# One ring of weight tiles for the whole second MLP, another order of operations inside a step, and last stores from two queues

## The chip, the cores and the metric

The kernel runs on one core of a Trainium2 chip. The metric is the device time of one execution in microseconds; the time given for a kernel is the median of its runs. Everything is computed in 32-bit floats. The engines are named as the profile names them: PE is TensorE, which multiplies matrices, PEld its weight loads; DVE is VectorE, ACT is ScalarE, POOL is GpSimd; SP is SyncE, whose queue (SPq) issues the DMAs.

## What is computed

An attention over memory slots, then two MLPs one behind the other. Cut to what matters:

```python
# q, k, v: 8 batches x 8 heads x 576 x 64; phi: 8 x 8 x 576 x 32
a = softmax(phi, axis=2)
k_m, v_m = einsum('bhsm,bhsd->bhmd', a, k), einsum('bhsm,bhsd->bhmd', a, v)
x = softmax(q @ k_m.T / 8) @ v_m            # brought to 4608 tokens x 512
h = x @ w_in                                # 512 x 2048
x = maximum(0.01 * h, h) @ w_out            # 2048 x 512
gate = sigmoid(x @ w_gate)                  # 512 x 1536
out = (gate * (x @ w_val)) @ w2_out         # 1536 x 512, result 4608 x 512
```

## The kernel before, in words

Every factor of a product is split into a high and a low part of TensorE's 32-bit format, and a product is the sum of three matmuls: high by high, low by high, high by low. The subtraction that gives the low part runs on VectorE or GpSimd, the copy that gives the high part on ScalarE.

The work has two stages. In the first, 256 steps go over 8 batches, 2 halves of 288 tokens and 16 blocks of 128 columns of the first MLP. One step of the loop over `steps` (L1354) holds, in this order: the split of an earlier block's activation (`fin`, L188 and L189), the first product of the block two steps ahead (`m1_in`, L836, and its activation L840), the operations of the attention units that are due (`unit_parts`), one tick of preparation, the units' work on TensorE (`ts_`), the weights of a later batch (`vw_pair`, L806), the second product (`m1_out`, L857), and the units' loads (`ls`). A unit is half of the heads of one batch; a table (`SCHED["chain"]` and its like) says in which step, counted from the unit's first, each of its parts is due. Among the parts: `v1` and `v2` take a maximum (L502, L515, L518); `v4` sums the exponentials in two operations on VectorE (L553, L555) and `t4` uses the sum on TensorE (L564, L573); `v5x` copies the result off with ScalarE (L603); `v10m` scales on GpSimd (L738), with its factor from the reciprocal L731.

The preparation is, in the first 30 steps, a tick that rewrites the first MLP's weights. From step 30 on it is the stash: the second MLP's weights are loaded, brought to a rounded form (L218, L222, L228 on ScalarE, L232 and L242 on VectorE, L250 on GpSimd), combined into seven blocks as Strassen's scheme wants them (L324 to L331), split (L337, L343), and stored to two DRAM tensors: `gvs` for `w_gate` and `w_val`, `w2s` for `w2_out`. The helper `run` takes a list of generators and goes around: one operation of the first, one of the second, and so on, until all are empty. Since engines work in the order in which operations are issued, this order is the order on each engine. The stash is the last generator of the list.

In the second stage the tokens are done in five pairs of blocks (480, 480, 448, 448 and 448 tokens wide). For a pair, three rounds (`th`) have each two column blocks (`j`), and for each of these one group of seven products for the gate and one for the value (`m2_group`, L1006, six matmuls a product). Between the rounds stands `m2_out` (L1142): 14 sums of products, (k, e) with k from 0 to 6 and e 0 or 1, each of six matmuls too. In what follows an operation is one such set of six matmuls with its tile of weights. A round's `m2_out` is issued behind the first group of the next round, the last round's behind its own four groups. Loads of the next pair's x (`x_load`, L907) are issued behind the first round's groups.

Weights come from DRAM through SP's queue. There are two sets of tiles. Five `wt` tiles of 512 KB hold two operations' weights each for `m2_group` and are refilled after the second one (`w_load`, L940). Four `ring` tiles of 256 KB serve `m2_out` and are refilled after each operation (`w2_load`, L952). Both wait for the matmuls that read the old content.

Each result of an `m2_out` operation is added to its sum on VectorE (L1152), or copied by ScalarE the first time (L1150); four PSUM banks take turns. In the plain order `OUT_SEQ` a bank comes again after four operations. The very last `m2_out` has an order of its own, `OUT_END`. After the last round the sums are transposed on VectorE (L1125) in chunks of 256 and 192 tokens and stored (`store`, L1182), four DMAs to a chunk and half; these operations wait in a list, `lazy`, from which a few are taken per `m2_out` operation: two in the last `m2_out`, one or two elsewhere. In the last `m2_out` two chunks of one half are stored once (4, 1) is done, the others after (6, 1), which is its last operation.

Of the kernel before, what the change touches and what calls it, by code (L numbers as in the profile page):

```python
# [119 lines left out]
def tile_kernel(  # L120
# [13 lines left out]
    nc = tc.nc  # L134
# [21 lines left out]
    NOP = 7  # L156
    IN_AT = IN_SEQ = (0, 2, 1, 3, 4, 5, 6)
    OUT_SEQ = [(k, e) for k in (0, 2, 1, 5, 4, 3, 6) for e in range(2)]
    OUT_END = [
        (0, 0), (2, 0), (1, 0), (0, 1), (5, 0), (2, 1), (4, 0), (1, 1), (3, 0), (5, 1), (6, 0), (4, 1), (3, 1), (6, 1),  # L160
    ]
    NOPS = NF2 * NOP
    SCALE = 1.0 / float(D) ** 0.5

# [16 lines left out]
    def f32(ap):  # L181
        return ap.bitcast(F32)
# [691 lines left out]
    xr = []  # L874
    xt = []
    xo = {}
    w_free = []
    w_at = {}
    w_next = [0]
    ops = []  # L880
    ring = []
    r_at = []
    sums = []
    banks = []
    stage2 = []
# [47 lines left out]
        t, h = xo[k, a], PAIRS[n][1]  # L933
        eng.tensor_sub(t[:, 1, :h], x_operand(n, k, a), f32(t[:, 0, :h]))  # L934

    def w_load():
        while w_free and w_next[0] < len(PAIRS) * NOPS // 2:
            m = w_next[0] % (NOPS // 2)
            t = w_at[w_next[0]] = w_free.pop(0)
            nc.sync.dma_start(out=f32(t), in_=gvs[:, 2 * m:2 * m + 2].rearrange("p o l a f -> p (o l a f)"))  # L940
            w_next[0] += 1

    def out_seq(n, th):
        return OUT_END if (n, th) == (len(PAIRS) - 1, NTH - 1) else OUT_SEQ

    r_next = iter([(th, e, k) for n in range(len(PAIRS)) for th in range(NTH) for k, e in out_seq(n, th)])

    def w2_load(t):
        x = next(r_next, None)
        if x:  # L950
            th, e, k = x
            nc.sync.dma_start(out=f32(t), in_=w2s[:, th, e, k])  # L952
            r_at.append(t)

    def out_open():
        for _ in range(TH // 2):
            ops.append([wtile("wo", [P, 2, 512], F32R, "op") for _ in range(NOP)])
        for _ in range(2):
            t = wtile("wo", [P, 2, TH // 2, 2, P], F32R, "ring")
            ring.extend(t[:, i] for i in range(2))  # L960
        for t in ring:
            w2_load(t)
        sums.extend(wtile("vw", [P, 2, 512], F32, "sum") for _ in range(4))
        banks.extend(ps_acc.tile([P, 512], F32, tag="acc", name="oacc") for _ in range(4))
        t = gp.tile([P, 2, 1024], F32, tag="ghl", name="turned", bufs=1)
        ts_ = [t[:, 0], t[:, 1], gp.tile([P, 1024], F32, tag="obuf", name="turned", bufs=1)]
        stage2.extend(t.rearrange("p (b q r) -> p b q r", q=4, r=32) for t in ts_)
# [24 lines left out]

    def m2_group(n, th, j, val):
        h = PAIRS[n][1]
        o0 = n * NOPS + NOP * (TH * th + 2 * j + val)
        direct = th == NTH - 1 and j == TH // 2 - 1

        def prod(k, bank, start):
            m, e = divmod(o0 + IN_AT[k], 2)
            w = w_at[m].rearrange("p (o l a f) -> p o l a f", o=2, l=2, a=2)[:, e]  # L1000
            i = 0
            for a in range(2):
                x = xo[k, a]
                for l, r in ((0, 0), (1, 0), (0, 1)):

                    nc.tensor.matmul(  # L1006
                        bank, w[:, l, a, :], x[:, r, :h], start=(start and i == 0), stop=(i == 5),
                        skip_group_check=not start,
                    )
                    i += 1  # L1010
            if e == 1:
                w_free.append(w_at.pop(m))
                w_load()

        def sg_tile():
            n_tmp[1] += 1
            return sgt[n_tmp[1] % len(sgt)][:, :h]

        def op_hi(k, x):
            return lambda: nc.scalar.copy(ops[j][k][:, 0, :h], x)  # L1020

        def op_lo(k, x):
            t = ops[j][k]
            return lambda: nc.vector.tensor_sub(t[:, 1, :h], x, f32(t[:, 0, :h]))  # L1024

        def sub(d, x, y):
            return lambda: nc.vector.tensor_sub(d, x, y)  # L1027

        def gate(s, c):
            return lambda: nc.scalar.activation(s, c, AF.Sigmoid)  # L1030

        def gated(s, c):
            return lambda: dve.tensor_mul(s, s, c)  # L1033

        def add(d, x, y):
            return lambda: dve.tensor_add(d, x, y)  # L1036

        def copy(d, x):
            return lambda: nc.scalar.copy(d, x)  # L1039

        dve = nc.vector
        turns = 0 if val else 2
        if val:
            b11, b12, b21, b22 = (sgs.pop(x) for x in range(4))
        else:
            s11, s12, s21, s22 = (sgs.setdefault(x, sg_tile()) for x in range(4))
        c11, c22, c12, r = (tmp(h) for _ in range(4))
        if val:
            t1, t2, t3, t4 = b11, tmp(h), b12, b21
        y = ps_a.tile([P, 512], F32, tag="a", name="ps_y")[:, :h]  # L1050
        prod(0, y, True)
        read(copy(c11, y), turns=turns)
        yield
        z = ps_h.tile([P, 512], F32, tag="h", name="ps_z")[:, :h]
        prod(2, z, True)
        read(copy(c22, z), turns=turns)
        yield
        prod(1, y, False)
        read(copy(c12, y), turns=turns)
        yield  # L1060
        x = ps_h.tile([P, 512], F32, tag="h", name="ps_x")[:, :h]
        prod(3, x, True)
        read(add(c11, x, c11), turns=turns)
        if val:
            gated(b11, c11)()
            after(1, op_hi(0, b11), op_lo(0, b11))
        else:
            after(1, gate(s11, c11))
        yield
        prod(4, y, False)  # L1070
        if val:
            read(copy(r, y), add(c22, r, c22), gated(b22, c22), turns=turns)
            if direct:
                op_hi(5, b22)()
            else:
                after(1, op_hi(5, b22))
        else:
            read(copy(r, y), add(c22, r, c22), turns=turns)
            after(1, gate(s22, c22))
        yield  # L1080
        prod(5, z, False)
        read(add(c12, z, c12), turns=turns)
        if val:
            gated(b12, c12)()
            sub(t1, b12, b11)()
            if direct:
                op_hi(2, t1)()
        else:
            after(1, gate(s12, c12))
        yield  # L1090
        prod(6, y, False)
        if not val:
            read(turns=turns)
            after(1, gate(s21, y))
        elif direct:
            read(gated(b21, y), turns=turns)
            op_lo(2, t1)()
            sub(t2, b22, t1)()
            op_hi(1, t2)()
            op_hi(3, b21)()  # L1100
            after(1, op_lo(1, t2), op_lo(5, b22))
            after(2, sub(t3, b22, b12), op_hi(4, t3))
            after(3, op_lo(3, b21), sub(t4, b21, t2), op_hi(6, t4))
            after(4, op_lo(4, t3))
            after(5, op_lo(6, t4))
        else:
            read(gated(b21, y), turns=turns)
            sub(t2, b22, t1)()
            after(1, op_hi(2, t1), op_hi(3, b21), op_lo(2, t1), op_lo(3, b21), op_lo(5, b22))
            after(2, op_hi(1, t2), sub(t3, b22, b12), op_lo(1, t2))  # L1110
            after(3, op_hi(4, t3), sub(t4, b21, t2))
            after(4, op_lo(4, t3))
            after(5, op_hi(6, t4))
            after(6, op_lo(6, t4))
        yield
# [3 lines left out]
    def m2_out(n, th, between):  # L1119
# [8 lines left out]

        def stored(t, x, m, st):
            f = lazy.pop()  # L1130
            lazy.append(lambda: (f(), store(t0 + t * h + x, m, st)))

        chunks = [(0, 256), (256, h - 256)]
        st = {}
        for k, e in out_seq(n, th):
            start = k in (0, 2, 3)
            b = banks[e if k in (0, 1, 4, 6) else 2 + e][:, :h]
            w = r_at.pop(0)
            i = 0
            for j in range(TH // 2):  # L1140
                for l, r in ((0, 0), (0, 1), (1, 0)):
# [2 lines left out]
                        skip_group_check=not start,  # L1144
                    )
                    i += 1
            w2_load(w)
            o = sums[SUM_OF[k]][:, e, :h]
            if th == 0 and k in (0, 2, 1, 6):
                read(lambda: nc.scalar.copy(o, b), turns=1)  # L1150
# [26 lines left out]
        n_st[0] += 1  # L1177
        return stage2[n_st[0] % len(stage2)]

    def store(n0, m, o):  # L1180
        for g in range(4):
            nc.sync.dma_start(  # L1182
                out=out[n0:n0 + m, P * g:P * g + P].rearrange("(b p) d -> p b d", p=32),
                in_=o[32 * g:32 * g + 32, 0:m // 32].rearrange("p b q r -> p b (q r)"),
            )


    with tc.manual_schedule():
# [154 lines left out]
            early.setdefault(6 + n, []).append((x_hi, (0, IN_SEQ[n // 2], n % 2)))  # L1343
            early.setdefault(7 + n, []).append((x_lo, (0, IN_SEQ[n // 2], n % 2, nc.vector)))

        def w_open():
            w_free.append(wtile("vw", [P, 2 * PC], F32R, "wt"))
            w_load()

        for n in range(5):  # L1350
            early.setdefault(4 if n == 0 else 16 + 2 * n, []).append((w_open, ()))
        first = m2_group(0, 0, 0, 0)
        held = None
        for i, (b, hf, fc) in enumerate(steps):  # L1354
# [19 lines left out]
                    convs[0].load()  # L1374
                    convs[1].load()
            else:
                vs.append(stash(i - i0 - 1))
            run(vs)
            for f, u in ts_:
                f(u)  # L1380
# [79 lines left out]
```

## Time and profile before

| | us |
|---|---|
| median of 3 runs | 1603.97 |
| lowest and highest | 1602.0, 1604.19 |
| the profiled execution | 1595.83 |
| its span, first to last instruction | 1594.1 |
| PE busy in it | 1530.8 (96%) |
| PEld busy in it | 1380.9 (87%) |
| DVE, ACT, POOL busy | 954.5, 820.8, 450.6 |

The profile is that of one execution. Busy time is the time in which an engine had an instruction running; matmuls overlap one another, so a busy PE isn't PE at its peak. "Idle before" an instruction is the time its engine did nothing ahead of it, and the releaser behind the arrow is what ended that. The first stage ends at about 784 us, the second with the last matmul near 1584 us.

### The profile page before, as it was taken

How to read it: one execution, taken by the hardware profiler on the slowest of the kernel's cores; microseconds unless marked ns; L12 is line 12 of the kernel's file. 1: busy time of each engine (PE TensorE's matmuls, PEld its weight loads, DVE VectorE, ACT ScalarE, POOL GpSimd, SP SyncE). 2: the span in 40 equal slices, each digit the busy share in tenths (PEclk: the TensorE clock that was granted, in tenths of full speed). 3: DMA queues.
4: the chain of work that ended last, by engine and by line, in shares of the span. 5: the costliest groups of instructions: out<-in, count | busy, mean ns of one | idle time of the engine just before them, and what ended most of it. 6: DMA issues, size and time to landing. Idle time of an engine off the chain costs nothing.

```text
span 1594.1 us, 28286 instructions
## 1 busy us (share of the span) xinstructions
PE 1530.8 (96%) x10508; PEld 1380.9 (87%) x10508; DVE 954.5 (60%) x1732; ACT 820.8 (51%) x1846; POOL 450.6 (28%) x445
## 2 busy tenths in 40 slices
PE   5789999999999999999999999999999999999997
PEld 2677888989999998999988888888999898989996
DVE  6886555556555556513065677558755875686466
ACT  5885555656566565645453355425543554255432
POOL 2986354444545444433200030002100200030000
PEclk8899999999999999999999999999999999999999
DMA  9823555544656565312276668666877687768774
GB/s 307 279 53 87 145 163 160 162 135 148 175 161 192 147 180 160 107 49 81 90 267 201 205 202 276 215 205 203 272 245 214 210 279 234 215 212 262 217 215 122
DMA packets 247529, 297.04 MB, mean 186 GB/s; under 512 B 98400, under 2 KB 172640, under 8 KB 247392
## 3 DMA queue, kind: packets, MB, share of 16 engines
q1 hardware_dynamic: 247392, 295.24, 60.4%
q8 instruction: 83, 1.36, 0.3%
q14 instruction: 54, 0.44, 0.1%
HBM read 243.27 MB, written 51.90 MB: 185 GB/s over the span
## 4 chain that ended last, share of the span: by engine, by line
PE 73%; DVE 5%; ACT 3%; DMA 2%; issue 1%; SPq 0%; DVEq 0%; ACTq 0%
PE ps_y L1006 18%; PE acc L857 17%; PE oacc L1142 13%; PE ps_z L1006 9%; PE ps_h L836 8%; PE ps_x L1006 5%; PE ps_vw L806 1%; DMA ring<-w2s 1%; DVE op L1024 1%; DVE sum L1152 1%; PE ps_kv L573 1%; DMA gvs<-hl 1%; DVE sg L1027 1%; DMA w2s<-hl 0%; DVE sg L1033 0%
## 5 line engine op out<-in xcount | busy, mean ns | idle before, releaser
L857 PE MATMUL acc<-ghl,wo 128*128 128x288 f32 x3072 | 463.9, 300 | 6.3 <-ACT obuf L866 2.2
L857 PEld LDWEIGHTS acc<-ghl,wo 128*128 128x128 f32 x3072 | 421.9, 189 | 32.9 <-issue 13.4
L1006 PE MATMUL ps_y<-xo,wt 128*128 128x448 f32 (+1 forms) x1440 | 332.3, 371 | 0.0
L189 POOL TENSOR_TENSOR ghl<-grs,ghl 128x288 fp32r<-128x288 f32 x250 | 217.7, 872 | 338.1 <-ACT ghl L188 244.9
L1006 PEld LDWEIGHTS ps_y<-xo,wt 128*128 128x128 f32 x1440 | 270.1, 188 | 30.3
L1142 PE MATMUL oacc<-op,ring 128*128 128x448 f32 (+1 forms) x1260 | 270.2, 372 | 4.1 <-DMA ring<-w2s 2.4
L1142 PEld LDWEIGHTS oacc<-op,ring 128*128 128x128 f32 x1260 | 234.6, 188 | 37.2 <-DVE sum L1152 3.8
L1039 ACT COPY tmp<-ps_y 128x448 f32<-128x448 f32 (+1 forms) x180 | 98.1, 545 | 267.1 <-PE ps_y L1006 267.1
L840 ACT ACTIVATE grs<-ps_h 128x288 f32<-128x288 f32 x256 | 105.7, 413 | 250.0 <-PE ps_h L836 228.7
L836 PE MATMUL ps_h<-at_hi,vw 128*128 128x288 f32 x1024 | 214.0, 297 | 3.6 <-ACT vw L188 2.8
L934 POOL TENSOR_TENSOR xo<-xr,xo 128x448 fp32r<-128x448 f32 (+1 forms) x28 | 38.4, 1404 | 594.4 <-DMA ring<-w2s 285.1
L836 PEld LDWEIGHTS ps_h<-at_hi,vw 128*128 128x128 f32 x1024 | 166.2, 190 | 5.0 <-ACT vw L188 3.6
L1006 PE MATMUL ps_z<-xo,wt 128*128 128x448 f32 (+1 forms) x720 | 169.8, 371 | 0.0
L1152 DVE TENSOR_TENSOR sum<-oacc,sum 128x448 f32<-128x448 f32 (+1 forms) x170 | 106.7, 634 | 97.5 <-PE oacc L1142 96.2
L836 PE MATMUL ps_h<-at_lo,vw 128*128 128x288 f32 x512 | 151.5, 296 | 0.0
L1006 PEld LDWEIGHTS ps_z<-xo,wt 128*128 128x128 f32 x720 | 135.1, 188 | 15.2
L1036 DVE TENSOR_TENSOR tmp<-ps_x,tmp 128x448 f32<-128x448 f32 (+1 forms) x60 | 38.1, 635 | 183.3 <-PE ps_x L1006 183.3
L1020 ACT CAST op<-sg 128x448 fp32r<-128x448 f32 (+1 forms) x180 | 103.4, 579 | 74.6 <-DVE sg L1027 44.7
L188 ACT CAST ghl<-grs 128x288 fp32r<-128x288 f32 x256 | 111.6, 436 | 2.0
L1024 DVE TENSOR_TENSOR op<-sg,op 128x448 fp32r<-128x448 f32 (+1 forms) x180 | 111.9, 645 | 0.5
L818 DVE TENSOR_TENSOR vw<-ps_vw,vw 128x256 fp32r<-128x256 f32 x112 | 39.7, 418 | 106.5 <-ACT vw L816 106.5
L836 PEld LDWEIGHTS ps_h<-at_lo,vw 128*128 128x128 f32 x512 | 96.9, 189 | 0.0
(173 smaller groups left out, 1755.6 us busy)
## 6 DMA issues: line engine op xcount, KB each, us to landing
wt<-gvs SPq DMA_DIRECT2D x210, 512.0 KB, 4.3
ring<-w2s SPq DMA_DIRECT2D x210, 256.0 KB, 2.9
gvs<-hl SPq DMA_DIRECT2D x84, 256.0 KB, 2.3
w2s<-hl SPq DMA_DIRECT2D x42, 256.0 KB, 2.4
x2s<-obuf SPq DMA_DIRECT2D x15, 576.0 KB, 3.6
win<-in_moe_w_in_dram SPq DMA_DIRECT2D x16, 512.0 KB, 10.0
wo_bits<-in_moe_w_out_dram SPq DMA_DIRECT2D x16, 512.0 KB, 10.4
q<-in_q_dram SPq DMA_DIRECT2D x224, 36.0 KB, 2.9
```

What stands on the lines that cost most here:

```text
L188: nc.scalar.copy(hi, raw)
L189: eng.tensor_sub(lo, raw, f32(hi))
L818: nc.vector.tensor_sub(w[:, 1, g], x, f32(w[:, 0, g]))
L836: nc.tensor.matmul(p[:, :HALF], w, x, start=(n == 0), stop=(n == 3 * NG - 1))
L840: nc.scalar.activation(gr, p[:, :HALF], AF.Prelu, alpha=0.01)
L857: nc.tensor.matmul(a[d][:, :HALF], w[:, ds_], x, start=(open_ and n == 0), stop=(close and n == 2),)
L1006: nc.tensor.matmul(bank, w[:, l, a, :], x[:, r, :h], start=(start and i == 0), stop=(i == 5), skip_group_check=not start,)
L1020: return lambda: nc.scalar.copy(ops[j][k][:, 0, :h], x)
L1024: return lambda: nc.vector.tensor_sub(t[:, 1, :h], x, f32(t[:, 0, :h]))
L1039: return lambda: nc.scalar.copy(d, x)
L1142: nc.tensor.matmul(b, w[:, j, l, :], ops[j][k][:, r, :h], start=(start and i == 0), stop=(i == 5), skip_group_check=not start,)
L1152: read(lambda: nc.vector.tensor_add(o, b, o), turns=2 if end and last else 1)
```

## The change

Three things are changed.

- The second MLP's weights all go through one ring. Where five tiles of 512 KB and four of 256 KB stood, there are 14 tiles of 256 KB in the same memory (ten from the five places tagged `vw`, four from the two tagged `wo`). One stream lists all operations in the order in which they are issued, products and sums of products mixed; each operation takes the oldest tile, and behind its matmuls that tile is loaded with the next content of the stream.
- In a step of the first stage with a stash, `run` first issues all operations of the units, and then the stash's by itself.
- `OUT_END` is dropped: the very last `m2_out` goes in the plain order. Its stores are issued in turn from SP and ScalarE, two DMAs of each chunk on either.

```diff
-    OUT_END = [
-        (0, 0), (2, 0), (1, 0), (0, 1), (5, 0), (2, 1), (4, 0), (1, 1), (3, 0), (5, 1), (6, 0), (4, 1), (3, 1), (6, 1),
-    ]
...
-    def w_load():
-        while w_free and w_next[0] < len(PAIRS) * NOPS // 2:
-            m = w_next[0] % (NOPS // 2)
-            t = w_at[w_next[0]] = w_free.pop(0)
-            nc.sync.dma_start(out=f32(t), in_=gvs[:, 2 * m:2 * m + 2].rearrange("p o l a f -> p (o l a f)"))
-            w_next[0] += 1
...
-    def w2_load(t):
-        x = next(r_next, None)
-        if x:
-            th, e, k = x
-            nc.sync.dma_start(out=f32(t), in_=w2s[:, th, e, k])
-            r_at.append(t)
+    def stream(n):
+        for th in range(NTH):
+            for j in range(TH // 2):
+                for val in range(2):
+                    o = NOP * (TH * th + 2 * j + val)
+                    for x in range(NOP):
+                        yield gvs[:, o + x].rearrange("p l a f -> p (l a f)")
+                    if th > 0 and (j, val) == (0, 0):
+                        yield from stream_out(th - 1)
+        yield from stream_out(NTH - 1)
+
+    def stream_out(th):
+        for k, e in OUT_SEQ:
+            yield w2s[:, th, e, k].rearrange("p j l f -> p (j l f)")
+
+    w_next = iter([x for n in range(len(PAIRS)) for x in stream(n)])
+
+    def w_load(t):
+        x = next(w_next, None)
+        if x is not None:
+            nc.sync.dma_start(out=f32(t), in_=x)
+            w_at.append(t)
+
+    def w_open(tag):
+        t = wtile(tag, [P, 2, 512], F32R, "wt")
+        for i in range(2):
+            w_load(t[:, i])
...
         for _ in range(2):
-            t = wtile("wo", [P, 2, TH // 2, 2, P], F32R, "ring")
-            ring.extend(t[:, i] for i in range(2))
-        for t in ring:
-            w2_load(t)
+            w_open("wo")
...
         def prod(k, bank, start):
-            m, e = divmod(o0 + IN_AT[k], 2)
-            w = w_at[m].rearrange("p (o l a f) -> p o l a f", o=2, l=2, a=2)[:, e]
+            t = w_at.pop(0)
+            w = t.rearrange("p (l a f) -> p l a f", l=2, a=2)
...
-            if e == 1:
-                w_free.append(w_at.pop(m))
-                w_load()
+            w_load(t)
...
-        for k, e in out_seq(n, th):
+        for k, e in OUT_SEQ:
...
-            w = r_at.pop(0)
+            wt = w_at.pop(0)
+            w = wt.rearrange("p (j l f) -> p j l f", j=TH // 2, l=2)
...
-            w2_load(w)
+            w_load(wt)
...
-    def store(n0, m, o):
+    def store(n0, m, o, end):
         for g in range(4):
-            nc.sync.dma_start(
+            (nc.scalar if end and g % 2 else nc.sync).dma_start(
...
         for n in range(5):
-            early.setdefault(4 if n == 0 else 16 + 2 * n, []).append((w_open, ()))
+            early.setdefault(4 if n == 0 else 16 + 2 * n, []).append((w_open, ("vw",)))
...
             else:
-                vs.append(stash(i - i0 - 1))
+                run(vs)
+                vs = [stash(i - i0 - 1)]
             run(vs)
```

## Rows read from the trace of the kernel before

**Rows 1.** Windows: each engine's busy us (instructions), PEclk, DMA share, GB/s.

```profile
180.00:784.00 604.00, 592.09 (x5450) 555.93 (x5449) 305.17 (x589) 346.69 (x908) 279.06 (x299) 1.00 0.48 142
784.00:1564.40 780.40, 777.66 (x3714) 693.61 (x3713) 500.79 (x881) 348.30 (x666) 56.44 (x44) 1.00 0.72 226
1583.80:1594.10 10.30, 0.00 (x0) 0.00 (x0) 1.79 (x5) 0.00 (x0) 0.00 (x0) 0.72 0.74 179
```

**Rows 2.** Waits of PE from 784 us on: us in total, times, longest.

```profile
PE oacc L1142 <- DMA ring<-w2s: 2.4, 4, 0.9
```

**Rows 3.** Timeline around one of those waits: start us, us, engine, line.

```profile
831.07 5.37 PE L1142 MATMUL oacc<-op,ring 128*128 128x480 f32 x24
...
836.86 8.32 PEld L1142 LDWEIGHTS oacc<-op,ring 128*128 128x128 f32 x39 [0.83 <-issue]
836.89 8.49 PE L1142 MATMUL oacc<-op,ring 128*128 128x480 f32 x38 [0.45 <-DMA ring<-w2s]
```

**Rows 4.** Line L952, the loads of `ring` tiles.

```profile
DMA to landing us min/median/max: 2.5/2.9/5.5
```

**Rows 5.** Timeline of SP's queue ahead of that wait.

```profile
822.53 2.43 SPq L907 DMA_DIRECT2D xr<-x2s  x4
```

**Rows 6.** Line L940, the loads of `wt` tiles.

```profile
DMA to landing us min/median/max: 3.2/4.3/8.6
```

**Rows 7.** Windows fed from `ring` tiles (first) and from `wt` tiles (second).

```profile
1053.00:1068.00 15.00, 15.00 (x71) 12.95 (x71) 7.88 (x12) 0.00 (x0) 0.00 (x0) 1.00 0.67 190
905.00:930.00 25.00, 25.00 (x117) 21.62 (x116) 14.22 (x24) 12.41 (x24) 0.00 (x0) 1.00 0.64 206
```

**Rows 8.** Waits of PE from 180 to 784 us.

```profile
PE ps_vw L806 <- ACT e L603: 4.2, 5, 1.8
PE ps_kv L564 <- DVE t L555: 2.7, 3, 1.9
PE ps_vw L806 <- DVE mx L515: 1.8, 1, 1.8
...
PE ps_m L524 <- DVE dg L518: 0.3, 2, 0.2
```

**Rows 9.** Timeline of DVE from 340 to 343 us.

```profile
341.17 0.67 DVE L242 SCALAR_TENSOR_TENSOR y<-y,raw 128x512 int32<-128x512 int32 x1
341.77 0.88 DVE L555 TENSOR_TENSOR t<-t,pht 64x128 f32<-64x128 f32 x1
```

**Rows 10.** Timeline of POOL from 233.5 to 237 us.

```profile
233.82 1.29 POOL L250 TENSOR_TENSOR y<-y,k 128x512 int32<-128x512 int32 x1
235.06 1.16 POOL L738 TENSOR_TENSOR e<-e,st 128x576 f32<-128x576 f32 x1
```

**Rows 11.** Timeline of DVE in the same stretch.

```profile
233.94 0.27 DVE L731 RECIPROCAL st<-st 128x18 f32<-128x18 f32 x1
```

**Rows 12.** Timeline of PE, last sums of products of the fourth pair.

```profile
1410.24 18.16 PE L1142 MATMUL oacc<-op,ring 128*128 128x448 f32 x84
```

**Rows 13.** Timeline of PE, last sums of products of the fifth pair.

```profile
1564.43 1.99 PE L1142 MATMUL oacc<-op,ring 128*128 128x448 f32 x9
...
1568.88 14.85 PE L1142 MATMUL oacc<-op,ring 128*128 128x448 f32 x72 [0.41 <-DVE sum L1152]
```

**Rows 14.** Timeline of SP's queue at the end.

```profile
1583.56 8.05 SPq L1182 DMA_DIRECT2D out_dram<-turned  x16
```

**Rows 15.** Timeline of DVE, fourth pair, 1420 to 1426 us.

```profile
1421.39 2.81 DVE L1152 TENSOR_TENSOR sum<-oacc,sum 128x448 f32<-128x448 f32 x5
```

**Rows 16.** Timeline of DVE at the end.

```profile
1582.56 0.62 DVE L1152 TENSOR_TENSOR sum<-oacc,sum 128x448 f32<-128x448 f32 x1
...
1583.77 0.62 DVE L1152 TENSOR_TENSOR sum<-oacc,sum 128x448 f32<-128x448 f32 x1
1584.31 1.28 DVE L1125 STREAM_TRANSPOSE turned<-sum 128x256 f32<-128x256 f32 x4
```

**Rows 17.** Window inside the last stores.

```profile
1585.00:1592.00 7.00, 0.00 (x0) 0.00 (x0) 0.59 (x3) 0.00 (x0) 0.00 (x0) 0.74 0.93 228
```

More of the change, by code (lines that the diff above doesn't have):

```diff
@@ L876, in tile_kernel @@
     xo = {}
-    w_free = []
-    w_at = {}
-    w_next = [0]
+    w_at = []
     ops = []
-    ring = []
-    r_at = []
     sums = []
@@ L934, in x_lo @@
         eng.tensor_sub(t[:, 1, :h], x_operand(n, k, a), f32(t[:, 0, :h]))
-    def w_load():
-        while w_free and w_next[0] < len(PAIRS) * NOPS // 2:
-            m = w_next[0] % (NOPS // 2)
-            t = w_at[w_next[0]] = w_free.pop(0)
-            nc.sync.dma_start(out=f32(t), in_=gvs[:, 2 * m:2 * m + 2].rearrange("p o l a f -> p (o l a f)"))
-            w_next[0] += 1
-    def out_seq(n, th):
-        return OUT_END if (n, th) == (len(PAIRS) - 1, NTH - 1) else OUT_SEQ
-    r_next = iter([(th, e, k) for n in range(len(PAIRS)) for th in range(NTH) for k, e in out_seq(n, th)])
-    def w2_load(t):
-        x = next(r_next, None)
-        if x:
-            th, e, k = x
-            nc.sync.dma_start(out=f32(t), in_=w2s[:, th, e, k])
-            r_at.append(t)
+    def stream(n):
[21 more added lines that the diff above has]
+            w_load(t[:, i])
     def out_open():
@@ L994, in m2_group @@
         h = PAIRS[n][1]
-        o0 = n * NOPS + NOP * (TH * th + 2 * j + val)
         direct = th == NTH - 1 and j == TH // 2 - 1
         def prod(k, bank, start):
-            m, e = divmod(o0 + IN_AT[k], 2)
-            w = w_at[m].rearrange("p (o l a f) -> p o l a f", o=2, l=2, a=2)[:, e]
+            t = w_at.pop(0)
+            w = t.rearrange("p (l a f) -> p l a f", l=2, a=2)
             i = 0
@@ L1130, in stored @@
             f = lazy.pop()
-            lazy.append(lambda: (f(), store(t0 + t * h + x, m, st)))
+            lazy.append(lambda: (f(), store(t0 + t * h + x, m, st, end)))
         chunks = [(0, 256), (256, h - 256)]
         st = {}
-        for k, e in out_seq(n, th):
+        for k, e in OUT_SEQ:
             start = k in (0, 2, 3)
             b = banks[e if k in (0, 1, 4, 6) else 2 + e][:, :h]
-            w = r_at.pop(0)
+            wt = w_at.pop(0)
+            w = wt.rearrange("p (j l f) -> p j l f", j=TH // 2, l=2)
             i = 0
@@ L1344, in tile_kernel @@
             early.setdefault(7 + n, []).append((x_lo, (0, IN_SEQ[n // 2], n % 2, nc.vector)))
-        def w_open():
-            w_free.append(wtile("vw", [P, 2 * PC], F32R, "wt"))
-            w_load()
         for n in range(5):
-            early.setdefault(4 if n == 0 else 16 + 2 * n, []).append((w_open, ()))
+            early.setdefault(4 if n == 0 else 16 + 2 * n, []).append((w_open, ("vw",)))
         first = m2_group(0, 0, 0, 0)
```

## The prediction

> **What bounds the kernel now.** I began with the busy time of each engine by stage. Before 180 us the program fills its pipeline and the change touches nothing. From 180 to 784 us (first MLP, beside attention and the stash) TensorE is busy 592.09 of 604 us; from 784 to 1564.4 us (second MLP) 777.66 of 780.4 us; the last 10.3 us pass with TensorE idle, and in them almost nothing but stores runs [rows 1]. So TensorE sets the pace, and an edit is worth what it takes out of TensorE's pauses (11.9 us in the first of these stretches, 2.7 in the second) or out of the 10.3 us at the end. The kernel's other work counts only where it ends one of those pauses. I then read who ended them, stretch by stretch. The sum is made against the profiled execution, 1595.83 us with a span of 1594.1; the median of the runs shown, 1603.97, is 8.1 us more, and I carry the same difference in us over to it.
>
> **Part 1, the ring.** TensorE waits for a `ring` tile four times, 2.4 us together, the longest 0.9 [rows 2]. One of the four: its pause is 0.45 us, and the weight load ahead of it stood still for 0.83 [rows 3]. A matmul's record lasts 0.17 us into the next one's, so the loss is idle plus about 0.17: 0.62 us here, 2.4 + 4 x 0.17 = 3.1 us for the four. The bounds are the idle alone, 2.4, and the weight loads' pause at the same ratio, 2.4 x 0.83 / 0.45 = 4.4.
> Why it waits: a tile is refilled when its six matmuls are done, and with four tiles it is wanted three operations later. An operation takes 6 x 0.2167 = 1.30 us at 480 columns (24 matmuls begin 831.07, the next ones were due 5.2 us later), so three give 3.9 us. A refill lands after 2.9 us in the median, but after up to 5.5 [rows 4]; the slow ones are those behind the four loads of x for the next pair, issued at 822.53 [rows 5]. With one ring of 14 a refill has thirteen operations: 16.9 us at 480 columns, 15.8 at 448. The slowest weight load of all took 8.6 us [rows 6]. I take all four waits as gone, and nothing is late behind them: the operands and banks of those operations were ready, since the matmuls after the pause run on without another.
> What it adds: 210 loads of 512 KB become 420 of 256 KB, so 210 more issues on SP. At the 0.50 us that an issue takes in the costliest run of them, 16 in 8.05 us [rows 14], an operation of 1.22 us spends under half of SP. They cost nothing as long as the ring holds; without that cover each late load would cost what the four waits cost now. SP is in order, and in the last sum of products of a pair the 16 stores wait there for VectorE's transposes with weight loads behind them; 16 x 0.50 = 8 us of issue spread over the operations stay below the 15.8 us of cover. Smaller loads need slightly more DMA: a stretch fed from the 256 KB tiles moves 190 GB/s at a busy share of 0.67, one fed from the 512 KB tiles 206 at 0.64 [rows 7], which is 284 against 322 GB/s at a full share. Need is near 215, so it fits.
> The Trainium skill ("DMA: Bandwidth & Descriptors", Rules for kernel authors) speaks against this part: for most bandwidth it wants at least 1 MiB in a DMA. The two shares agree in direction; by that rule alone the part would be priced as a loss, but the loss falls on DMA time that is free here.
>
> **Part 2, units ahead of the stash.** From step 30 on, a step's stash operation used to be dealt out in turn with the units' operations; now it stands behind all of them on each engine. What TensorE waited for from 180 to 784 us [rows 8]: for VectorE's second sum L555 three times, 2.7 us; for VectorE's maximum L515 once, 1.8; for the scaled identity L518 twice, 0.3; for ScalarE's L603 five times, 4.2.
> Ahead of 342.8 us the order on VectorE is seen: the stash's L242 stands before L555 [rows 9], the unit's reduction L553 before both. Without L242 between them L555 starts at 341.17 instead of 341.77, 0.60 us earlier. The longest of the three waits, 1.9, loses 0.6; the other two, 0.8 together, are each under such a step and go whole, with 0.17 us of overlap each: 0.6 + 0.8 + 0.34 = 1.7 us. For L515: GpSimd does the stash's L250 from 233.82 for 1.29 us, then the unit's L738 [rows 10], whose input L731 was ready at 233.94 + 0.27 = 234.21 [rows 11]; with L250 behind it, L738 starts about 0.85 us earlier, and with it VectorE's transpose and L515: 0.85 us. The two short L518 waits go: 0.3. L603 is alone in its unit's step and comes ahead of that step's stash already, so its 4.2 us stay. Sum 2.9 us.
> Nothing of this kind is without a price: the stash's operations end later in their step, and a unit operation that waits for another engine now holds them up. Their output is read only from DRAM, hundreds of us later. Behind them on ScalarE and GpSimd stand the next step's cast and subtraction of the activated block, which TensorE wants one step (some 2.6 us) later; that is the cover. Bounds: all waits of [rows 8] gone, 9.0 us; or as much lost as is gained at the nearest waits, -2.9.
>
> **Part 3, the end.** The fifth pair now takes the plain order of products. The fourth pair has it already, with the same operand preparation: its 84 matmuls take 18.16 us [rows 12], while the fifth's begin at 1564.43 and, with three pauses, the last 72 end at 1568.88 + 14.85 = 1583.73, so 19.30 [rows 13]: TensorE gains 1.14 us. But VectorE doesn't. In the fourth pair the sixth to tenth addition run back to back from 1421.39, 0.54 us apart [rows 15], so the eighth starts at 1422.47, and from there the fifth pair adds two transposes to each addition, 1.22 us a turn by the turns at the end [rows 16]. The fourteenth addition then starts 6 x 1.22 later, and the last transpose ends 0.54 + 1.28 after that, at 1431.6, or 21.4 us after the matmuls began. Before, it was 1584.31 + 1.28 - 1564.43 = 21.2. The gain on TensorE is lost again on VectorE.
> What moves is the first eight stores. Their last transposes now follow the eleventh addition, at 16.8 us from the start, on the old clock 1581.2, where the old 16 stores began at 1583.56 [rows 14]. The other eight can begin at about 1585.4 and are no longer behind the first. Two prices for them. From the first issue of the old stores to the end of the span it is 10.5 us, of which 16 issues take 8.05 [rows 14]; the other 2.5 are the last store's way. By issue alone, four on each queue at 0.50 us and 2.5 behind them, the end lies at 1585.4 + 2.0 + 2.5 = 1589.9: a gain of 4.2. By the DMA engines: in the old stores they are 0.93 busy at 228 GB/s [rows 17], so two queues find little free bandwidth. Eight stores, four of 128 and four of 96 KB, are 0.918 MB, or 4.0 us: 1585.4 + 4.0 + 2.5 = 1591.9, a gain of 2.2. I take 2.2, since 0.93 is the row on the stretch itself. Bounds 0 and 4.2.
> The Trainium skill ("DMA: Bandwidth & Descriptors", Issuing engines are not separate DMA queues) says that queues of several engines share the same 16 DMA engines and that a second queue saves only issue time. The row of 0.93 agrees with it; by the rule this part's second queue is worth nothing by itself.
>
> **Sum:** 3.1 + 2.9 + 2.2 = 8.2 us. Profiled 1595.83 - 8.2 = 1587.6; median 1603.97 - 8.2 = 1595.8.
>
> **Rivals.**
> (a) The order of units is worth nothing, the pauses only move: 5.3 us left, 1598.7. For it: the ScalarE waits, the largest, aren't touched. Against: the stash instruction stands visibly between L553 and L555.
> (b) The order helps more, because ScalarE's wait L603 shrinks with the backlog: 4.2 us and its five overlaps of 0.17 on top, 13.3 in all, 1590.7.
> (c) The ring brings new waits. Stores and loads of x come in bursts on the one queue, and a product group of the first layer, which never waited for weights, now shares its tiles. At the measured longest ring wait with overlap, 1.1 us, in five or six places, 6 us of the gain go: 1601.8. Against it: 15.8 us of cover and 8.6 at worst.
> (d) Only the ring pays: the stores share busy engines and the order is neutral, 3.1 us, 1600.9.
> (e) Slower: the stash's operations, pushed to the end of the step, hold up the next step's cast and subtraction (L188), and TensorE waits for `ghl` in the first MLP. Twelve units run beside the stash or after it, each over about 20 steps. It decides from 8.5 us on (5.3 + 3.2), 0.7 us for a unit; at 1.2 us for a unit, 14.4 us are lost and 5.3 won: 1613.1. For it: ScalarE and GpSimd are busy 346.69 and 279.06 of 604 us [rows 1], and one L738 keeps GpSimd for 1.16 us [rows 10]. Against: the 2.6 us of cover.
>
> **How the numbers follow.** A measurement of this kernel can tell 0.2%, 3.2 us, from no change. Chances: the forecast 0.50, (a) 0.15, (b) 0.07, (c) 0.13, (d) 0.07, (e) 0.08. Faster takes the forecast, (a) and (b): 0.72; same (c) and (d): 0.20; slower (e). The range of 8 in 10 leaves (e) and the ends of (b) and (c) out: from 1590.0, where (b) lies, to 1602.0, (c).
>
> **What would show it.** Right: no wait for a weight tile in the second MLP; the three waits for L555 shorter or gone, L603 as before; the first eight stores issued two operations before the last matmul; about 8 us from the last matmul to the end. Wrong: waits for `wt` in product groups after stores or loads of x; more idle time of TensorE for `ghl` between 180 and 784 us; a DMA share in the last stores far under 0.9 with an earlier end, which would make the second queue worth more than I say.

## The result, and the profile after

| | before | changed |
|---|---|---|
| median of the runs, us | 1603.7 (4 runs) | 1587.09 (4 runs) |
| lowest to highest | 1602.0 to 1604.19 | 1584.55 to 1590.2 |
| the profiled execution | 1595.83 | 1584.55 |
| its span | 1594.1 | 1582.7 |

The ratio is 0.9895, with a 95% interval of 0.9876 to 0.9914: 16.8 us faster, of which 8.2 were forecast, and the median lies under the range of 1590.0 to 1602.0. The two profiled executions are only 11.3 us apart. So two questions stood: what in the kernel gained more than its step in the prediction, and why the medians gained more than the profiles.

These windows of the changed kernel answer to [rows 1] and [rows 17] (same columns; the first product of the second MLP now begins at 779.53 us instead of 782.39, the last sum of products at 1556.44 instead of 1564.43, so the windows end earlier):

```profile
180.00:781.10 601.10, 591.90 (x5451) 555.93 (x5450) 305.20 (x589) 346.70 (x908) 281.26 (x299) 1.00 0.49 143
781.10:1556.40 775.30, 774.75 (x3714) 694.61 (x3713) 501.69 (x881) 348.08 (x666) 56.36 (x44) 1.00 0.77 230
...
1575.00:1581.00 6.00, 0.00 (x0) 0.00 (x0) 1.51 (x5) 0.00 (x0) 0.00 (x0) 0.80 0.95 241
```

TensorE does the same matmuls with 9.2 us of pauses in the first stretch (11.9 before) and 0.6 in the second (2.7 before). The waits of TensorE from 180 to 781 us, beside [rows 8] (the lines have moved by three: L603 is L600 here, L555 is L552, L515 is L512):

```profile
PE ps_vw L803 <- ACT e L600: 4.1, 5, 1.8
PE acc L854 <- POOL ghl L186: 2.1, 5, 0.5
PE ps_vw L803 <- DVE mx L512: 1.1, 1, 1.1
PE ps_kv L561 <- DVE t L552: 0.7, 1, 0.7
```

From 781 us on no wait of a matmul is left in the list. What stays there are short ones of the weight loads, of which this is the longest:

```profile
PEld oacc L1139 <- DVE sum L1149: 4.1, 9, 0.5
```

The weight loads of the one ring (beside [rows 4] and [rows 6]): the slowest took 8.3 us and nobody waited for it.

```profile
DMA to landing us min/median/max: 2.6/3.0/8.3
```

The reordered step, on VectorE at 341 us and on GpSimd at 235 us (beside [rows 9] and [rows 10]): L552 now stands right behind the reduction and ahead of the stash's L239, and the unit's L735 ahead of the stash's L247.

```profile
340.07 1.08 DVE L550 TENSOR_REDUCE t<-e 128x128 f32<-128x512 f32 x1
341.19 0.28 DVE L552 TENSOR_TENSOR t<-t,pht 64x128 f32<-64x128 f32 x1
341.39 0.68 DVE L239 SCALAR_TENSOR_TENSOR y<-y,raw 128x512 int32<-128x512 int32 x1
```

```profile
235.07 1.16 POOL L735 TENSOR_TENSOR e<-e,st 128x576 f32<-128x576 f32 x1 [0.41 <-DVE st L728]
236.18 1.26 POOL L247 TENSOR_TENSOR y<-y,k 128x512 int32<-128x512 int32 x1
```

And the end, beside [rows 13], [rows 14] and [rows 16]: the last sums of products in one run, the stores from 15.9 us after its start instead of 19.1, eight on either queue.

```profile
1556.44 17.97 PE L1139 MATMUL oacc<-op,wt 128*128 128x448 f32 x84
...
1566.93 1.68 DVE L1149 TENSOR_TENSOR sum<-oacc,sum 128x448 f32<-128x448 f32 x3
...
1572.34 6.89 SPq L1179 DMA_DIRECT2D out_dram<-turned  x8
1572.35 6.93 ACTq L1179 DMA_DIRECT2D out_dram<-turned  x8
...
1573.61 0.59 DVE L1149 TENSOR_TENSOR sum<-oacc,sum 128x448 f32<-128x448 f32 x1
...
1574.73 0.59 DVE L1149 TENSOR_TENSOR sum<-oacc,sum 128x448 f32<-128x448 f32 x1
1575.23 1.28 DVE L1121 STREAM_TRANSPOSE turned<-sum 128x256 f32<-128x256 f32 x4
```

### The profile page after: what moved, and what is told of

The parts are those of the page before. It is cut to its first block, busy times and chain, and to the rows that moved or that the text cites. A ratio compares the mean times of both kernels' runs of the same rounds, so it can differ in the third digit from the quotient of the medians.

```text
span 1582.7 us, 28978 instructions
## 1 busy us (share of the span) xinstructions
PE 1527.7 (97%) x10508; PEld 1381.5 (87%) x10508; DVE 955.1 (60%) x1732; ACT 820.4 (52%) x1846; POOL 452.4 (29%) x445
## 4 chain that ended last, share of the span: by engine, by line
PE 74%; DVE 5%; ACT 2%; DMA 2%; issue 1%; POOL 0%; SPq 0%; DVEq 0%; ACTq 0%; POOLq 0%
PE ps_y L1004 19%; PE acc L854 18%; PE oacc L1139 13%; PE ps_z L1004 9%; PE ps_h L833 8%; PE ps_x L1004 5%; PE ps_vw L803 1%; DVE op L1020 1%; DVE sum L1149 1%; PE ps_kv L570 1%; DMA kv<-in_v_dram 1%; DVE sg L1023 1%; DMA w2s<-hl 0%; DVE sg L1029 0%; DVE tmp L1032 0%
## 5 line engine op out<-in xcount | busy, mean ns | idle before, releaser
L186 POOL TENSOR_TENSOR ghl<-grs,ghl 128x288 fp32r<-128x288 f32 x250 | 219.8, 881 | 332.3 <-ACT ghl L185 237.9
L1139 PE MATMUL oacc<-op,wt 128*128 128x448 f32 (+1 forms) x1260 | 268.6, 372 | 0.6
L1139 PEld LDWEIGHTS oacc<-op,wt 128*128 128x128 f32 x1260 | 235.2, 188 | 31.5 <-DVE sum L1149 4.1
```

The costliest lines, as they stand in the source:

```text
L186: eng.tensor_sub(lo, raw, f32(hi))
L1139: nc.tensor.matmul(b, w[:, j, l, :], ops[j][k][:, r, :h], start=(start and i == 0), stop=(i == 5), skip_group_check=not start,)
```

## The experiments

### The kernel before once more, and each part alone

Four kernels on one chip, beside 23 runs of the kernel before with a median of 1602.35 us (1598.34 to 1607.97).

**Before again.** Nothing edited.

> The kernel before once more, profiled on the chip of the next three runs. Theory A (the profiled execution of before was simply a quiet one, and its waits for the ring are longer in others): this execution takes longer than 1595.83 us, and TensorE's waits for a ring tile come to more than 2.4 us in four, by about the excess. Theory B (the ring's waits are always near 3.1 us with overlap, and the remaining time lies in the pace of the matmuls): the waits stay at 2 to 3 us, and the runs of 84 matmuls at 448 columns take more than 17.03 us in some stretches.

1598.01 us. TensorE's waits in the second MLP, beside [rows 2]:

```profile
PE oacc L1142 <- DMA ring<-w2s: 4.6, 5, 1.3
PE oacc L1142 <- DVE op L1024: 1.5, 4, 0.5
```

The ring's waits are 4.6 us, not 2.4, and this execution still lies under every one of the 23 runs. Theory A holds, and part of B with it, as the next profiles show.

**Part 1 alone.** The changed kernel with these edits taken back:

```diff
-                run(vs)
-                vs = [stash(i - i0 - 1)]
+                vs.append(stash(i - i0 - 1))
...
-            (nc.scalar if end and g % 2 else nc.sync).dma_start(
+            nc.sync.dma_start(
...
-        for k, e in OUT_SEQ:
+        for k, e in out_seq(n, th):
```

> Part 1 alone: one ring of 14 tiles, the old order of units and stash, OUT_END and one store queue. My prediction's step: 3.1 us faster (0.2%). Theory A: 8 to 12 us faster, since before's waits are longer on this chip. Theory B: 3 to 5 us, with no wait for a weight tile in the profile either way.

Ratio 0.9958 (0.9943 to 0.9972): 6.7 us faster (4.5 to 9.1), between the two theories. No wait for a weight tile is left.

**Part 2 alone.** The kernel before with

```diff
-                vs.append(stash(i - i0 - 1))
+                run(vs)
+                vs = [stash(i - i0 - 1)]
```

> Part 2 alone: the units' operations ahead of the stash's. My prediction's step and both theories: 2.9 us faster, the second stage beginning 2.9 us earlier. Rival: the order also shifts the stage 2 waits, and the gain is over 5 us.

Ratio 0.9975 (0.9963 to 0.9988): 4.0 us, 1.9 to 5.9; the 2.9 fit, and the rival of over 5 isn't excluded. In the traces the stretch from the 481st to the 2281st matmul of the first MLP's second product (some 187 to 614 us) takes 427.6, 427.8 and 427.2 us in the kernel before (twice) and in part 3 alone, and 425.2, 424.6 and 425.5 with the new order (part 2 alone, the changed kernel, the changed kernel once more): 2.4 us less by the means, 427.5 against 425.1.

Two other profiles with the old order took longer in this stretch: 431.1 us in part 1 alone and 429.0 in the run with the loads of x earlier (below). In both, the granted clock was at its lower level for a while behind a pause that the new order shortens: from 342.6 us, where TensorE waits for L555, and from 237.9 us, where it waits for L515. None of the eight profiles with the new order has such a drop in the stretch. Over all six profiles with the old order (the sixth, two rings dealt out otherwise, takes 428.7) the mean is 428.6, over seven with the new one (without the variant that moves a unit's copy) 425.3: 3.2 us.

The second stage itself begins at 781.06 us here, not clearly earlier than the 782.39 and 780.89 of before: behind the stretch, at 620.49, this execution waits 2.31 us for L603, and its clock drops too.

**Part 3 alone.** The kernel before with

```diff
-        return OUT_END if (n, th) == (len(PAIRS) - 1, NTH - 1) else OUT_SEQ
+        return OUT_SEQ
...
-            nc.sync.dma_start(
+            (nc.scalar if end and g % 2 else nc.sync).dma_start(
```

> Part 3 alone: the plain order in the very last sum of products, and stores from two queues. From the two traces, from the last sum's first matmul to the end of the span: 26.3 us against 29.7, 3.4 us faster; my prediction's step was 2.2. The ring still has four tiles here, so weight loads stand on SP's queue until about 5 us before the end; if these matter to the first stores the gain is nearer 2.2.

Ratio 0.9978 (0.9967 to 0.9989): 3.5 us, 1.8 to 5.3. From the last sum's first matmul to the end of the span it takes 26.2 us, as in the changed kernel, so the weight loads on SP's queue don't matter there. The three parts sum to 14.2 us.

This profile, with the four tiles still in place, also shows what a late refill costs beside its wait. Its timeline of TensorE at 1166.84 us (the first refilled tile of the third pair) and, much later, a whole round of sums:

```profile
1166.84 14.14 PE L1142 MATMUL oacc<-op,ring 128*128 128x448 f32 x60 [1.89 <-DMA ring<-w2s]
...
1528.79 17.52 PE L1142 MATMUL oacc<-op,ring 128*128 128x448 f32 x84
```

beside it a whole round of sums of the changed kernel:

```profile
1205.48 17.19 PE L1139 MATMUL oacc<-op,wt 128*128 128x448 f32 x84
```

and windows of part 3 alone ahead of the wait, behind it, and after that (PEclk is the third number from the end, 1.00 being 2.4 GHz and 0.50 being 1.2):

```profile
1160.00:1164.00 4.00, 4.00 (x22) 3.70 (x21) 0.96 (x2) 2.25 (x5) 0.00 (x0) 1.00 1.02 417
...
1168.50:1171.80 3.30, 3.30 (x11) 2.92 (x11) 0.00 (x0) 0.98 (x2) 0.00 (x0) 0.55 0.31 87
1172.00:1180.00 8.00, 8.00 (x41) 7.26 (x40) 7.22 (x13) 0.23 (x1) 0.00 (x0) 1.00 0.69 196
```

Ahead of the wait the DMA engines are full (1.02). TensorE stood still for 1.89 us, and in the window from 1.7 us behind the pause on the granted clock is mostly at its lower level: 11 matmuls in 3.3 us instead of some 16. And the 84 matmuls of the later round take 17.52 us where the changed kernel's round needs 17.19. The last matmul's record lasts 0.37 us, so from one start to the next it is (17.52 - 0.37) / 83 = 206.6 ns against (17.19 - 0.37) / 83 = 202.7. I call this the pace. The slower pace is in every profile with four ring tiles, over several rounds each.

So I compared the second MLP as a whole, from the first product's first matmul to the last sum's first:

| kernel | us | TensorE's waits for a weight tile |
|---|---|---|
| four ring tiles: before, before again, part 2 alone, part 3 alone | 782.0, 785.4, 786.4, 790.1 | 2.4 to 4.7 us in 4 to 7 |
| one ring of 14: part 1 alone, the changed kernel, once more; below: a unit's copy earlier, the old last order | 776.9 in each of the five | none |
| one ring of 14, below: one queue; one pause (1.3 us of waits for VectorE) | 779.5; 781.4 | none |

Beside the 776.9, the old rings take 5.1 to 13.2 us more, not 3.1, and a different amount in each execution. Of the 13.2, the waits are 4.7 us, with overlaps of 0.17 us 5.9. An estimate of the rest from the same trace: some 1030 matmuls at the slower pace, 4.0 ns each, make 4.1 us, and 3.4 us at half the clock lose 1.7; 1.5 us stay open. Not all of this is the rings': two of the seven profiles with one ring of 14 (the last row) have the slower pace too, for some 670 matmuls or 2.7 us, without a wait for a weight tile.

### The changed kernel and three variants of it

One chip, 9 runs of before with a median of 1602.59 us.

**The changed kernel once more.**

> The changed kernel once more, beside the variants of it that follow on the same chip. If the three parts measured alone (6.7, 4.0 and 3.5 us by their ratios) add up: 14 us faster than before, and runs of 84 matmuls at 448 columns take 17.03 us throughout the second MLP. If the parts help each other: 16 us or more.

1584.71 us (1584.09 to 1587.12, 5 runs), ratio 0.989 (0.9869 to 0.9912). The parts' 14.2 us and the whole's 16.8 and 17.6 lie within one another's intervals; whether the parts help each other is not settled. The 84 matmuls of a round at 448 columns take the expected 17.03 us in the first two rounds of each pair, from start to start; in the third they take 17.6 to 18.0.

**A unit's copy one step earlier.**

```diff
-           'v5x': 8,
+           'v5x': 7,
```

> The changed kernel with ScalarE's copy of a unit's sums (v5x) one step earlier, in the step of the reciprocal, for the batches from the fourth on. It now comes due in the step behind a block's end, where ScalarE still has four copies of the block's output. My reading: the waits of TensorE for that copy (4.5 us in six) go, and with the longest, near 620 us, the drop of the granted clock behind it: 5 to 7 us faster than the changed kernel. Rival: the copy then waits for the reciprocal in its own step and holds up the cast behind it on ScalarE, and the time stays within 2 us.

1579.6 us (1578.34 to 1582.77, 5 runs), ratio to before 0.9861 (0.9836 to 0.9885): 5.1 us faster than the changed kernel by the medians, and no run of either reaches into the other's. It beats both kernels. The waits for the copy (4.1 us in five in the changed kernel) are gone from the list of waits from 180 to 781 us, which now begins:

```profile
PE acc L854 <- POOL ghl L186: 2.1, 5, 0.5
PE ps_vw L803 <- DVE mx L512: 1.1, 1, 1.1
```

That is the reading, not the rival. The gain doesn't hang on the clock: the changed kernel once more has no drop near 620 us in its profile either and begins its second stage at 779.26 us, this variant at 773.60.

**Six tiles.**

```diff
-        for n in range(5):
+        for n in range(2):
...
-        for _ in range(2):
-            w_open("wo")
+        w_open("wo")
```

> The changed kernel with 6 tiles in the one ring instead of 14 (two places of vw and one of wo), nothing else changed. Cover of five operations, 6.1 us at 448 columns. Theory A (depth is what counts, and pauses cost more than their idle time): waits for a weight tile behind the loads of x and behind the stores of each pair, stretches of 206.7 ns per matmul behind them, a drop of the granted clock behind the longest; 8 to 15 us slower than the changed kernel. Theory B (putting both kinds through one ring is what counts, whatever its depth): within 3 us of the changed kernel.

1618.06 us, ratio to before 1.0097 (1.0069 to 1.0126), 33 us slower than the changed kernel: theory A, at more than twice the size that I gave it. Depth is what counts, and one ring without it doesn't help. The sums of products, which had three operations of cover before and have five now, no longer wait; the waits have moved to the products, whose five tiles of two operations gave them eight:

```profile
PE ps_y L1003 <- DMA wt<-gvs: 13.0, 7, 3.0
PE ps_z L1003 <- DMA wt<-gvs: 7.4, 7, 1.4
PE ps_x L1003 <- DMA wt<-gvs: 2.2, 4, 0.9
```

The second MLP takes 812.5 us, 35.6 more than with 14 tiles, for 22.6 us of waits.

**One pause.**

```diff
+            spare = tmp(h) if (n, th, j) == (2, NTH - 1, TH // 2 - 1) else None
...
-            after(1, op_hi(0, b11), op_lo(0, b11))
+            if (n, th, j) == (2, NTH - 1, TH // 2 - 1):
+                after(1, op_hi(0, b11), *[sub(spare, b11, b11) for _ in range(3)], op_lo(0, b11))
+            else:
+                after(1, op_hi(0, b11), op_lo(0, b11))
```

> The changed kernel with three subtractions into an unused tile on VectorE, ahead of the first low part in the last product group of the third pair; the results stay the same. Theory A (a pause of TensorE itself changes the pace behind it): one pause of 1 to 2 us near 1247 us in the second MLP, no wait for a weight tile, and the matmuls behind it at 206.7 ns instead of 202.7 until the next pause of this size or the end, up to 6 us in all. Theory B (the pace belongs to the late weight loads): the pause costs its own 1 to 2 us and the pace stays at 202.7.

1587.84 us, one run. Neither theory as it stood. TensorE's timeline: the third pair's second round ahead of the pause, the pause, the fourth pair's first round behind it.

```profile
1206.44 17.52 PE L1143 MATMUL oacc<-op,wt 128*128 128x448 f32 x84
...
1251.90 2.92 PE L1143 MATMUL oacc<-op,wt 128*128 128x448 f32 x12 [1.08 <-DVE op L1020]
...
1312.20 17.19 PE L1143 MATMUL oacc<-op,wt 128*128 128x448 f32 x84
```

The slow pace was there before the pause, without any wait for weights, from the start of the 448-column pairs on, and behind the pause of 1.08 us it was gone. But the changed kernel with one store queue (below), which has no such pause, shows the same in the same two rounds:

```profile
1208.12 17.52 PE L1139 MATMUL oacc<-op,wt 128*128 128x448 f32 x84
...
1312.04 17.19 PE L1139 MATMUL oacc<-op,wt 128*128 128x448 f32 x84
```

There too the slow pace begins with the first pair of 448 columns and ends in the last sums of products of the third pair, and no wait of TensorE is listed in them. So the slow pace doesn't belong to late loads alone, and that the made pause ended it isn't shown. What sets the pace isn't shown either.

### Where the lateness came from, and the end

One chip, 13 runs of before with a median of 1604.32 us.

**Two rings, dealt out otherwise.** The kernel before with three `wt` tiles and eight `ring` tiles:

```diff
-        for n in range(5):
+        for n in range(3):
...
+        for _ in range(2):
+            t = wtile("vw", [P, 2, TH // 2, 2, P], F32R, "ring")
+            ring.extend(t[:, i] for i in range(2))
```

> The kernel before with the same memory dealt out otherwise: three tiles of 512 KB (six operations) for the product groups and eight of 256 KB for the sums of products, still two rings; nothing else changed. Theory A (depth where the refills are late is what counts): seven operations of cover, 8.5 us, end the waits in the first sums of products, and the five to six operations left to the product groups bring few new ones: 3 to 7 us faster than before. Theory B (only one ring for both kinds serves, since each kind's refills stand still while the other works): waits for wt in the product groups take their place, within 2 us of before.

1637.35 us, ratio 1.0207 (1.0182 to 1.0231): 33 us slower, far outside both theories. The waits in the sums of products are gone, as A had it, but I had counted the other side wrongly. A `wt` tile is refilled when its second operation is done, so of three tiles the refill is wanted four operations later, 4.9 us at 448 columns, and a load of 512 KB lands as the line of these loads says, with the waits for them above it:

```profile
  PE ps_y L1009: 18.0, 9
  PE ps_x L1009: 6.6, 4
  PE ps_z L1009: 4.2, 5
...
DMA to landing us min/median/max: 3.4/4.4/8.6
```

**The loads of x earlier.** The kernel before, with the loads behind the pair's second group:

```diff
+                        if more and (th, j, val) == (0, 0, 1):
+                            for c in range(KD):
+                                x_load(n + 1, c)
...
-                if more and th == 0:
-                    for c in range(KD):
-                        x_load(n + 1, c)
```

(That is two groups earlier than before, not the three that the expectation says.)

> The kernel before with the four loads of the next pair's x issued three product groups earlier, behind the first group of the pair instead of the fourth; rings, order and end as before. If these loads are what makes the first refill late: no wait for a ring tile in the first sums of products of pairs one to four, and about half to two thirds of the ring's 6.7 us: 3 to 5 us faster than before. If the refills are late for want of bandwidth anyway: the waits stay.

Ratio 0.9965 (0.995 to 0.998): 5.6 us faster (3.2 to 8.0), beside the ring's 6.7. Of the waits of TensorE in the second MLP this one for a weight tile is left:

```profile
PE oacc L1142 <- DMA ring<-w2s: 0.7, 1, 0.7
```

The four loads of x just ahead of the sums of products were what made most of the refills late. With them elsewhere even four tiles nearly do: the second MLP takes 780.7 us. In the four profiles with four ring tiles that the table of the second MLP lists, 11.7 of the 15.8 us of waits for a weight tile stand 11 to 20 us behind loads of x. The other 4 us don't, nor does the one left here. The longest of them, in before again, is in the fifth pair, which has no loads of x:

```profile
1538.30 2.66 PE L1142 MATMUL oacc<-op,ring 128*128 128x448 f32 x12 [1.26 <-DMA ring<-w2s]
```

The load it waited for was issued at 1533.43 and took 4.7 us to land, where the median of these loads is 3.0 in that profile. Why isn't shown.

**One queue, and the old last order.** The changed kernel with all last stores on SP:

```diff
-            (nc.scalar if end and g % 2 else nc.sync).dma_start(
+            nc.sync.dma_start(
```

> The changed kernel with all last stores on SP's queue again. From the last sum's first matmul to the end of the span it was 26.3 us in the changed kernel and 29.7 before. By the share of the DMA engines (0.93 busy with one queue) my prediction gave the second queue nothing: then 26 to 27 us here. By issue: the last eight issues take 4 us instead of 2 and begin when the first are through: 28 us or more.

and the changed kernel with `OUT_END` again, for the very last sums and the stream alike:

> The changed kernel with OUT_END, the old order of the very last sum of products, and the stores from two queues. If the earlier first half of the stores is what pays: 29 us or more from the last sum's first matmul to the end of the span. If the second queue pays: 27.5 us or less.

From the last sum's first matmul to the end of the span: 26.4 us with one queue (1559.85 to 1586.2), 29.0 with the old order and two queues (1556.63 to 1585.6), 26.3 and 26.1 with both edits, 29.6 and 29.9 with neither, each from one execution. (Part 1 alone, which has neither, takes 31.2: behind the pauses of the old order its clock is at the lower level for 3.4 us from 1567.9.) SP's queue in the first:

```profile
1575.75 8.14 SPq L1179 DMA_DIRECT2D out_dram<-turned  x16
```

and in the second:

```profile
1575.75 6.55 SPq L1185 DMA_DIRECT2D out_dram<-turned  x8
```

Half as many issues take 6.55 us on one queue when the other issues as well. The order pays 2.7 to 3.5 us, the second queue 0.1 to 0.9, the clock's drop left out.

## Why the prediction was wrong

**The step that failed** is "I carry the same difference in us over to it". For the profiled execution the prediction had 1587.6 and 1584.55 came, 3 us off: by the profiles the first MLP, the second MLP and the end gained 2.9, 5.1 and 3.4 us, where parts 2, 1 and 3 were forecast at 2.9, 3.1 and 2.2. For the median it added the 8.1 us by which before's runs stand above its profile; the changed kernel's median stands 2.5 above its own. These 5.6 us are the larger part of the 8.7 by which 1595.8 missed 1587.09.

That difference was no constant around the kernel. Both profiled executions of before were shorter than every run beside them (1595.83 where the runs begin at 1602.0, 1598.01 where they begin at 1598.34). Before's 23 runs on one chip spread over 9.6 us, the changed kernel's four over 5.7 and its five on another chip over 3.0, and the profiles with four ring tiles differ by 8.1 us within the second MLP alone. Part 3 alone comes nearest to a usual execution of before: it took 1600.16 us with an end 3.4 us shorter, so an estimate with the old end is 1603.6, about before's median, and its second MLP is 8.1 us longer than in before's first profile. That speaks for much of the difference being the very cost that part 1 removes. No execution of before near its own median was traced, so how much isn't shown.

**Part 1, forecast 3.1 us (2.4 to 4.4), measured 6.7 (4.5 to 9.1).** The mechanism was right: late refills, three quarters of their waits behind the loads of x (the run with earlier loads), cover of thirteen operations against 8.3 us at worst, no new wait, smaller loads at no cost. The size was off twice. It came from one execution, and that was the one with the shortest waits of four; and "the loss is idle plus about 0.17" left out what stands behind the waits: a lower granted clock in one profile, the slower pace in all, though not by late loads alone. Six tiles show the same on a larger scale, 22.6 us of waits for 35.6.

**Part 2, forecast 2.9, measured 4.0 (1.9 to 5.9) by runs and 2.4 by traces, 3.2 with the two in which the clock fell.** Right, and by its steps: L555 lost 2.0 of 2.7 us of idle time (1.4 forecast), L515 0.7 of 1.8 (0.85 forecast), the L518 waits went, L603 stayed at 4.1. What I had left at nothing came too: the waits for `ghl` from GpSimd rose from 0.8 us in two to 2.1 in five, rival (e) in small. The clock's drops behind these pauses were in no term.

**Part 3, forecast 2.2, measured 3.5 (1.8 to 5.3) by runs and 3.4 by traces.** The earlier first half pays and the second queue next to nothing, as argued from the busy share of 0.93; the Trainium skill ("DMA: Bandwidth & Descriptors", Issuing engines are not separate DMA queues) has it so, and 0.1 to 0.9 us agrees with it. The term that was off is VectorE's time. I took 1.22 us a turn from [rows 16], but there VectorE was waiting for TensorE, whose six matmuls of an operation take 6 x 0.2027 = 1.22; back to back a turn takes 1.12 (additions at 1573.61 and 1574.73). And the eighth addition, the last of the three from 1566.93, began 11.6 us after the first matmul, where I had 12.2 from the fourth pair. So the last transpose ended 20.1 us after the first matmul, not 21.4.

Of the rivals, none came. The Trainium skill's rule on large DMAs ("DMA: Bandwidth & Descriptors", Rules for kernel authors) didn't decide: the share rose from 0.72 to 0.77 in the second MLP, and no one waited.

## What to carry to other kernels

A ring's depth is its cover in operations, counted from the refill's issue to the next use, and it has to hold against the slowest landing in the queue's worst burst, not the median; a refill that comes only every second operation loses one of them. A pause of TensorE can cost more than its idle time (35.6 us for 22.6 with six tiles), so price it as a lower bound. Where a kernel's executions spread by more than the gain that is looked for, look at several before taking the gap between one profile and the median for a constant.

## What was not expected of the hardware

The same matmuls of 448 columns run at 202.7 or at 206.7 ns each for hundreds of them, at an unchanged granted clock. In two of seven profiles with one ring of 14 the pace was slow from the first of these pairs on and became fast in the last sums of the third, in one of them behind the made pause, in the other without a listed wait; at 480 columns the mean was 216.7 wherever nothing waited. What decides it was not found.

The granted clock fell behind some pauses of about 2 us and not behind others. In the profile of part 1 alone TensorE waits 2.35 us until 342.98; from 342.6 to 349.4 the clock is at its lower level:

```profile
340.00:342.50 2.50, 0.64 (x5) 0.40 (x3) 2.50 (x5) 2.47 (x6) 1.42 (x2) 1.00 0.00 0
342.60:349.40 6.80, 6.42 (x64) 5.68 (x65) 2.71 (x6) 0.35 (x2) 2.49 (x3) 0.50 0.49 152
```

In the run with the loads of x earlier it waits 1.83 us until 236.90, and behind it:

```profile
238.00:241.20 3.20, 3.20 (x13) 3.20 (x14) 2.42 (x6) 1.53 (x5) 0.81 (x1) 0.50 0.00 0
```

In the changed kernel run once more a pause of 1.98 us at 620 us was followed by no drop; in its first profile one of 1.78 us at the same place was. The variant with the earlier copy, which has no such pause there, has no drop there either.
